# The same steps of a hand-ordered kernel in another order, from step 440 to about 1206

## The chip, the cores and the metric

The kernel runs on one core of a Trainium2 chip. The core has a matrix engine (PE, with a separate unit that loads weights, PEld), a vector engine (DVE), a scalar engine (ACT), a further engine for element-wise work (POOL, also called GpSimd), and SP, which issues the transfers. Each engine works through its own instructions in the order in which the program gives them, and an instruction that waits for another engine holds up all that stand behind it on its own engine. The metric is the time of one execution in microseconds (us). The profile reports a span, the time between the first and the last instruction, which is a little shorter.

## The reference

```python
def _attn_ref(x, a, B, C):                      # x (4, 8, 768, 32), B and C (4, 8, 768, 16)
    log_a = np.log(np.clip(a, 1e-06, 1.0))
    for c in range(nc):                         # chunks of 32 tokens
        cum = np.cumsum(la, axis=-1)
        L = np.exp(cum[:, :, :, None] - cum[:, :, None, :]) * causal
        CB = np.einsum('bhin,bhjn->bhij', Cc, Bc)
        y_intra = np.einsum('bhij,bhjd->bhid', CB * L, xc)
        y_inter = np.einsum('bhin,bhnd->bhid', Cc, state) * np.exp(cum)[:, :, :, None]
        y[:, :, sl] = y_intra + y_inter
        state = decay_full * state + np.sum(Bx, axis=2)
...
def _moe_ref(x, w_gate, w_val, w_out, rms_g):   # x (3072, 256), 256 -> 1536 -> 256
    rms = np.sqrt(np.mean(x * x, axis=-1, keepdims=True) + 1e-06)
    xn = x / rms * rms_g
    g = xn @ w_gate
    silu = g * (1.0 / (1.0 + np.exp(-g)))
    return (silu * (xn @ w_val) @ w_out)
```

A scan over chunks with a carried state (first function) gives y; heads and head elements of a token are put side by side as 256 features, and each token goes through a norm, a gated pair of projections to 1536, and a projection back to 256. All is float32.

## The kernel before

The 3072 tokens are worked on in six blocks (0 to 5) of 512. While the projections of one block run, the scan and the norm of the next block are computed beside them. The two projections of a block are made with a scheme of seven products in place of eight on 2 x 2 parts (half blocks of 256 tokens, pairs of 128-wide slices of the 1536 features, j = 0 to 5). The projection back is made with a fast scheme of twenty products on sums of the hidden values and sums of the weights. Block 0 has a plainer path of its own.

The whole program is a list of 1667 steps written out by hand in a string, `order`, of the form `block:kind.numbers`. A loop at the end of the function takes them one by one and calls the function of that kind, which emits its instructions. The list thus sets the order on every engine at once: two steps that use the same engine run there in the order of the list, and steps on different engines run beside each other as far as data and buffers allow. Nothing re-orders them later.

```python
    for step in order.split():
        ...
        if blk == "0":
            first_kinds[kind](*numbers)
        else:
            kinds[kind](int(blk), *numbers)
```

The kinds that the text uses, with their lines:

- `P.k.j` (L965, `product_gv`): product k of the seven for pair j, on PE: four matmuls of 128x256 into one of two pairs of PSUM banks, "gate" and "val", two passes each; it reads the normed tokens `xn` or their differences `tx`. `take.k.j` (L971) is the ACT copy of the gate bank after product 1, 6 or 7; the next product that adds onto this bank waits for it. `C.c.j` (L977, DVE) adds the copy to the val bank; `silu.c.j` (L215, ACT) applies the gate function; `hid.c.j` on DVE or `hidp.c.j` on POOL (L990) multiplies into the hidden values.
- `u.n` on DVE or `up.n` on POOL (L1060): the n-th of 16 sums of hidden values. `O.k.h` (L1086): half h of product k of the twenty, four matmuls of 128x128 on PE. `w.n` (L1113 a copy on ACT, L215 a negated copy on ACT, L1117 an addition on DVE) brings a product into the output tile `ob`; `put` (L1122, SP) stores 128 rows of it. `o.f` (L997) is the plain projection back of block 0, eight PE instructions each, for f = 0 to 11.
- The scan of the next block: `T`, `Tt`, `Td` (L558 DVE, L1194 ACT, L587 DVE) make turned operands, `g` (L613) their products on PE, `L` and `L1` (L646) their decay on DVE, `S` (L692 to L702) the states on DVE, `y` (L750, L678) the outputs on PE. `spread` (L514, SP) loads decays, `sub` or `subp` (L520, DVE or POOL) subtracts, `ex` (ACT with two masks on POOL, L507) is the exponential, `scale2` or `scale2p` (L539) scales, `bc`, `x` and `sq2` (SP) load, `dT` (L580, SP) loads decays for `Td`.
- The norm of the next block: `sq` (squares on ACT, L215, then an addition on POOL, L802), `yt` (ACT copies of y, L818 and L821), `ms` (sums over the features on PE, L834), `rs` (root on ACT and its store, "roots", L847), `rb` (four loads that spread it over the partitions, L852), `xn` (two DVE operations, L861), `tx` or `txp` (differences, L942, DVE or POOL). For these steps the block number is that of the block whose projections run: `1:ms` is the norm of block 2.
- `two` or `twop` (L1042), `cw` or `cwp` (L934): sums of weights on DVE or POOL. ACT holds one set of functions at a time; going from silu to exponential and logarithm or back emits a table load (L207 to silu, L209 to exponential). `exps` and `table` ask for one early.

The sums and the factors of the twenty products are tables; where a p follows a kind's name, the same operation is handed to POOL:

```python
    def sum_h(blk, n, engine=nc.vector):
        o, in0, in1 = SUMS[n]
        engine.tensor_tensor(out=hidden_or_sum(o), in0=hidden_or_sum(in0),
        ...
        "u": sum_h, "up": lambda blk, n: sum_h(blk, n, nc.gpsimd), "O": product_o, "w": total_o, "put": put_tile,
```

Of the kernel before, what the change touches and what calls it, by code (L numbers as in the profile page):

```python
# [20 lines left out]
def kernel(  # L21
# [1231 lines left out]
    def of_chunk(n, fn):  # L1253
# [79 lines left out]
        1:Tt.1.0 1:Td.1 1:C.12.3 0:sq2.2.0.3 1:T.0.0 1:Td.0 1:hidp.12.0 1:spread.1 1:hid.11.2 0:o.10
        1:P.3.2 1:bc.0 1:T.1.0 1:take.1.5 1:scale2p.0 1:sq2.1.0 1:C.12.2 1:sq2.1.3 0:o.11
        1:silu.12.3 1:two.10 1:P.6.5 2:bc.0 1:P.6.4 0:put.0 1:silu.12.2 1:P.2.4 0:put.3 1:C.11.4
        0:put.2 1:hid.12.2 0:put.1 1:P.2.5 1:take.6.4 1:P.7.4 1:P.5.4 1:take.6.5 1:C.11.5 1:take.7.4
        1:silu.11.4 1:P.7.5 1:take.7.5 1:g 1:sq2.0.0 1:P.4.5 2:bc.1 1:P.5.5 1:hid.22.2 1:silu.11.5
        1:sub.2 1:hid.12.3 1:C.22.4 1:hid.11.4 1:P.4.4 1:two.6 1:subp.1 1:silu.21.5 1:sub.0
        1:hid.11.5 1:silu.22.4 1:hidp.22.4 1:L1.3 1:hid.21.5 1:up.1 1:O.2.0 1:O.2.1 1:twop.7
        1:C.22.5 1:L 1:silu.22.5 1:O.15.0 1:silu.21.4 1:L1.2 1:P.3.5 1:hid.21.4 1:O.15.1 1:y.0 1:w.0  # L1340
        1:w.2 1:sq2.0.1 1:up.0 1:O.3.0 2:dT.0 1:sq2.0.3 1:C.12.5 1:silu.12.5 1:hid.12.5 1:sq2.1.1
        1:u.3 1:O.3.1 1:O.0.0 1:O.0.1 1:P.3.4 1:w.4 1:u.2 1:sq2.1.2 1:O.17.0 1:O.17.1 1:w.5 2:S.0
        1:O.6.0 1:O.6.1 1:u.4 1:u.5 1:u.9 1:up.6 1:w.10 1:x.1 1:C.12.4 1:O.16.0 1:silu.12.4
        1:hid.12.4 1:hid.22.5 1:u.7 1:O.4.0 1:O.4.1 1:sq2.0.2 1:O.9.0 1:O.9.1 1:u.10 1:O.16.1 1:ex.0
# [7 lines left out]
        2:sub.3 1:ex.1 1:ex.2 1:w.25 2:scale2.1 2:take.1.1 2:ex.3 2:P.6.1 2:C.11.0 2:P.2.1  # L1352
        2:take.6.0 2:P.7.0 2:C.11.1 2:L 2:take.6.1 2:P.7.1 2:take.7.0 2:silu.11.1 2:L1.3 1:put.0
        2:P.5.1 2:take.7.1 2:C.22.1 2:dT.1 2:Td.1 2:L1.2 2:P.4.0 2:silu.21.0 2:P.5.0 2:C.22.0
        2:silu.11.0 2:spread.0 2:P.4.1 2:silu.21.1 2:silu.22.0 2:hidp.22.0 2:hid.21.1 2:P.3.1
        2:C.12.1 2:hid.21.0 2:y.0 2:P.1.3 2:take.1.3 2:P.1.2 2:hid.11.1 2:take.1.2 2:P.3.0
        2:hid.11.0 2:silu.22.1 2:C.12.0 2:silu.12.0 1:put.1 2:hid.12.0 2:silu.12.1 2:hidp.12.1
        2:P.2.3 3:scale2p.1 2:C.11.3 2:silu.11.3 2:P.6.3 2:take.6.3 2:P.6.2 3:S.0 3:dT.1 2:P.2.2
        2:C.11.2 2:sq2.1.3 2:sq2.0.0 2:take.6.2 2:P.5.3 2:silu.11.2 2:P.7.2 2:take.7.2 1:put.3
        2:table 2:P.7.3 2:hid.11.2 2:P.5.2 2:C.22.2 2:hid.11.3 2:take.7.3 2:P.4.2 2:silu.21.2  # L1360
        2:sq2.1.2 1:put.2 2:hid.21.2 2:P.4.3 2:C.22.3 2:silu.22.3 2:hid.22.3 2:silu.21.3 2:sq2.1.1
        3:T.0.1 2:silu.22.2 2:hid.22.2 2:x.1 2:y.1 3:S.1 2:sq 2:yt 2:P.1.5 2:hid.21.3 2:P.3.2
# [18 lines left out]
        3:sq2.0.1 2:w.19 3:silu.21.0 3:hid.22.0 3:P.4.1 3:scale2.0 3:silu.21.1 3:sq2.1.1 3:L1.3
        2:w.21 2:w.24 3:hid.21.0 3:silu.11.0 2:w.23 2:O.10.0 2:O.10.1 3:P.2.1 2:w.25 3:hid.21.1
        4:dT.1 3:C.11.1 3:P.1.4 3:take.1.4 3:P.1.3 3:L1.2 3:y.0 3:P.5.1 3:sub.1 3:C.22.1 3:take.1.3
        3:P.6.3 3:P.2.3 3:silu.22.1 3:hidp.22.1 3:silu.11.1 2:put.3 3:take.6.3 3:P.3.1 3:P.6.4
        3:P.7.3 3:silu.12.0 3:hid.12.0 3:C.11.3 3:silu.11.3 3:hid.11.3 3:C.12.1 3:P.5.3 3:hid.11.0
        4:T.1.1 3:take.6.4 3:P.7.4 3:take.7.3 3:C.22.3 3:P.2.4 3:P.4.3 3:silu.12.1 3:hid.12.1
        3:take.7.4 3:P.4.4 3:x.1 3:P.3.3 3:silu.22.3 3:C.11.4 3:hid.11.1 3:silu.21.4 4:S.0
        3:silu.21.3 2:put.2 3:C.12.3 3:silu.12.3 3:hidp.12.3 3:table 3:hid.21.4 3:hid.21.3
        3:silu.11.4 3:P.5.4 3:y.1 3:subp.3 3:P.1.5 3:C.22.4 3:silu.22.4 3:take.1.5 3:hidp.22.4
        3:hid.22.3 4:S.1 3:P.1.2 3:P.3.4 3:take.1.2 3:C.12.4 3:sq 3:silu.12.4 3:sq2.0.2 3:P.6.5  # L1390
        3:take.6.5 3:P.2.5 2:put.0 4:T.0.1 4:Tt.0.1 3:C.11.5 3:P.2.2 3:C.11.2 3:yt 3:P.6.2
        3:take.6.2 3:silu.11.2 3:hid.11.4 3:P.7.5 3:P.5.5 3:take.7.5 3:silu.11.5 3:hidp.12.4 2:put.1
        3:C.22.5 3:silu.22.5 3:P.7.2 3:hid.11.2 3:take.7.2 3:P.4.5 3:silu.21.5 3:u.0 3:P.5.2 3:P.4.2
        3:hidp.22.5 4:Tt.0.0 3:hid.21.5 3:hid.11.5 3:O.2.0 3:sq2.0.3 3:O.2.1 3:O.15.0 3:C.22.2
        3:silu.21.2 3:O.15.1 3:hid.21.2 3:P.3.2 3:silu.22.2 3:u.1 3:u.3 3:C.12.2 3:P.3.5 3:C.12.5
        3:u.4 3:hid.22.2 3:w.0 3:w.2 3:O.3.0 3:O.3.1 3:O.0.0 4:Tt.1.1 3:silu.12.2 4:T.1.0 3:up.2
        3:O.0.1 3:hidp.12.2 3:O.6.0 3:silu.12.5 3:ms 3:w.4 3:O.17.0 3:O.17.1 3:rs 3:w.5 3:w.10
        3:hidp.12.5 3:O.6.1 3:up.5 3:rb 3:O.16.0 3:O.16.1 3:u.6 4:Tt.1.0 3:w.1 3:w.3 3:u.7 3:u.8
# [93 lines left out]
```

## Time and profile before

| | before |
|---|---|
| median of 3 runs | 392.15 us (392.1 to 392.5) |
| profiled execution, its own time | 392.46 us |
| its span | 390.6 us |
| matmul instructions, and their weight loads | 3805 and 3805 |
| instructions on DVE, ACT, POOL | 620, 471, 160 |
| bytes read and written in HBM | 23.69 MB, 3.74 MB |

The costliest groups of instructions on each engine but PE are these (line, engine, operation, operands, shapes, count; busy time in the span and mean ns of one; idle time of the engine just before them and what ended most of it):

```profile
L977 DVE TENSOR_TENSOR c<-val,p 128x512 f32<-128x512 f32 x99 | 67.6, 687 | 46.8 <-PE val L965 32.3
L971 ACT COPY p<-gate 128x512 f32<-128x512 f32 x99 | 57.0, 582 | 60.5 <-PE gate L965 58.4
L990 POOL TENSOR_TENSOR hid<-c 128x256 f32<-128x256 f32 x33 | 26.8, 814 | 94.0 <-ACT c L215 79.1
```

Idle time of an engine that others wait for matters; idle time of DVE, ACT or POOL that PE does not wait for costs nothing. So the views to read are those of PE: its busy share, what it waits for, the chain of waits that leads back from the last instruction, and the timeline around the places where one block's norm must be ready for the next block's first products.

### The profile page before, as it was taken

How to read it: one execution, taken by the hardware profiler on the slowest of the kernel's cores; microseconds unless marked ns; L12 is line 12 of the kernel's file. 1: busy time of each engine (PE TensorE's matmuls, PEld its weight loads, DVE VectorE, ACT ScalarE, POOL GpSimd, SP SyncE). 2: the span in 40 equal slices, each digit the busy share in tenths (PEclk: the TensorE clock that was granted, in tenths of full speed). 3: DMA queues.
4: the chain of work that ended last, by engine and by line, in shares of the span. 5: the costliest groups of instructions: out<-in, count | busy, mean ns of one | idle time of the engine just before them, and what ended most of it. 6: DMA issues, size and time to landing. Idle time of an engine off the chain costs nothing.

```text
span 390.6 us, 9632 instructions
## 1 busy us (share of the span) xinstructions
PE 383.9 (98%) x3805; PEld 329.0 (84%) x3805; DVE 290.4 (74%) x620; ACT 227.2 (58%) x471; POOL 140.7 (36%) x160
## 2 busy tenths in 40 slices
...
DMA packets 109940, 28.05 MB, mean 72 GB/s; under 512 B 94824, under 2 KB 103752, under 8 KB 109896
## 3 DMA queue, kind: packets, MB, share of 16 engines
...
q8 instruction: 30, 0.49, 0.6%
...
HBM read 23.69 MB, written 3.74 MB: 70 GB/s over the span
## 4 chain that ended last, share of the span: by engine, by line
PE 87%; DVE 9%; issue 2%; DMA 1%; ACT 0%; POOL 0%; DVEq 0%; POOLq 0%
PE gate L965 29%; PE o L1086 22%; PE val L965 22%; PE o L997 5%; PE y L750 3%; PE g L613 1%; DVE wgv L243 1%; DVE m L237 1%; DVE m L234 1%; DVE hid L912 1%; PE g L606 1%; PE e L474 1%; PE y L678 1%; DMA L<-rowd 1%; DVE L L652 1%
## 5 line engine op out<-in xcount | busy, mean ns | idle before, releaser
L977 DVE TENSOR_TENSOR c<-val,p 128x512 f32<-128x512 f32 x99 | 67.6, 687 | 46.8 <-PE val L965 32.3
L971 ACT COPY p<-gate 128x512 f32<-128x512 f32 x99 | 57.0, 582 | 60.5 <-PE gate L965 58.4
L965 PE MATMUL gate<-tx,wgv 128*128 128x256 f32 x264 | 65.5, 381 | 0.0
L990 POOL TENSOR_TENSOR hid<-c 128x256 f32<-128x256 f32 x33 | 26.8, 814 | 94.0 <-ACT c L215 79.1
L215 ACT ACTIVATE c<-c 128x256 f32<-128x256 f32 x99 | 39.8, 415 | 31.8 <-DVE c L977 31.7
L965 PEld LDWEIGHTS gate<-tx,wgv 128*128 128x128 f32 x264 | 49.3, 190 | 7.5 <-ACT p L971 1.0
L990 DVE TENSOR_TENSOR hid<-c 128x256 f32<-128x256 f32 x66 | 32.5, 500 | 9.7 <-ACT c L215 9.5
L1117 DVE TENSOR_TENSOR ob<-ob,o 128x128 f32<-128x128 f32 (+1 forms) x90 | 24.3, 297 | 19.7 <-PE o L1086 13.7
L1086 PE MATMUL o<-two,hid 128*128 128x128 f32 x280 | 36.7, 277 | 0.0
L1086 PEld LDWEIGHTS o<-two,hid 128*128 128x128 f32 x280 | 34.6, 192 | 1.2 <-issue 0.4
L965 PE MATMUL val<-tx,sw 128*128 128x256 f32 x132 | 34.0, 381 | 0.0
L965 PE MATMUL val<-xn,wgv 128*128 128x256 f32 x132 | 33.3, 380 | 0.0
L965 PE MATMUL val<-xn,sw 128*128 128x256 f32 x132 | 33.3, 380 | 0.0
L965 PE MATMUL gate<-tx,sw 128*128 128x256 f32 x132 | 33.0, 381 | 0.0
L965 PE MATMUL gate<-xn,wgv 128*128 128x256 f32 x132 | 32.9, 384 | 0.0
L507 POOL TENSOR_SCALAR_AFFINE_SELECT L<-L 64x512 f32<-64x512 f32 x32 | 23.3, 729 | 21.0 <-ACT L L215 19.7
L965 PEld LDWEIGHTS val<-tx,sw 128*128 128x128 f32 x132 | 24.7, 190 | 3.7 <-DVE c L977 0.2
L965 PEld LDWEIGHTS val<-xn,wgv 128*128 128x128 f32 x132 | 24.9, 190 | 3.4
L965 PEld LDWEIGHTS gate<-tx,sw 128*128 128x128 f32 x132 | 24.5, 190 | 3.8 <-ACT p L971 0.4
L965 PEld LDWEIGHTS gate<-xn,wgv 128*128 128x128 f32 x132 | 24.0, 190 | 3.9 <-DVE hid L912 0.3
L965 PEld LDWEIGHTS val<-xn,sw 128*128 128x128 f32 x132 | 24.4, 190 | 3.2 <-issue 0.2
L215 ACT ACTIVATE e<-e,kinks 128x512 f32<-128x512 int16 (+1 forms) x36 | 26.0, 722 | 1.2
...
## 6 DMA issues: line engine op xcount, KB each, us to landing
...
```

The source lines that it names most:

```text
L215: nc.scalar.activation(**operands)
L234: nc.vector.tensor_scalar(out=m, in0=hi, scalar1=0xFFFFF, scalar2=0x100000, op0=ALU.bitwise_and, op1=ALU.bitwise_or)
L237: nc.vector.scalar_tensor_tensor(out=f, in0=lo.bitcast(U32), scalar=2.0 ** -32, in1=m, op0=ALU.mult, op1=ALU.add)
L507: nc.gpsimd.affine_select(out=L[r], in_=L[r], pattern=[[0, L.shape[1]], [1, HC]], compare_op=ALU.is_ge, fill=0.0, base=0, channel_multipli ...
L750: nc.tensor.matmul(out=y[2 * k + u][rows, (2 * n + i) * HC:(2 * n + i + 1) * HC], start=(k, u, rows.start) not in opened, stop=True, skip_ ...
L965: nc.tensor.matmul(out=dst[:, half[w]], lhsT=lhsT, rhs=rhs, start=(k in (1, 2, 5) and w == 0), stop=True, skip_group_check=True)
L971: nc.scalar.copy(out=t, in_=Xs[j])
L977: nc.vector.tensor_tensor(out=t, in0=Zs[j], in1=a, op=ALU.add)
L990: engine.tensor_tensor(out=hid[:, 2 * j + c // 10 - 1, c % 10 - 1], in0=u, in1=src[:, half[1]], op=ALU.mult)
L997: nc.tensor.matmul(out=o, lhsT=hid[:, f, k // 2, (k % 2) * P:(k % 2 + 1) * P], rhs=wo[:, f], start=opens, stop=(f == NF - 1), skip_group_c ...
L1086: nc.tensor.matmul(out=Os[blk, b][:, place * P:(place + 1) * P], lhsT=hidden_or_sum(u)[:, g], rhs=rhs, start=(blk, b) not in opened, stop= ...
L1117: nc.vector.tensor_tensor(out=o, in0=o, in1=src, op=ALU.add if what[0] == "+" else ALU.subtract)
```

## The change

Only the string `order` changes. Its first 439 steps and those from the 1207th on stand as they were. The steps between (from block 1's later projections to block 4's first ones) are the same set in another order, which was made with the lengths of the operations varied a little at random. Of these 767 steps 58 also change the engine that does them: 33 go from DVE to POOL (17 `u`, 6 `hid`, 4 `sub`, 3 `tx`, a `cw`, a `two`, a `scale2`) and 25 from POOL to DVE (8 `hid`, 7 `u`, 3 `sub`, 3 `scale2`, 3 `tx`, a `two`). The 107 P, 114 O, 5 o, 3 g, 6 y and 3 ms steps of the part and the 251 transfers of the whole kernel are the same in kind and number. The steps 0:o.7 to 0:o.11, spread up to the 505th place before, all stand before the 469th after. In parts, with what is left out marked by "...":

```diff
-        1:w.1 3:bc.1 1:y.1 1:w.6 1:w.3 2:T.0.1 2:Tt.0.0 1:u.11 2:S.1 1:O.18.0 1:O.18.1 1:u.12
-        1:O.8.0 1:O.8.1 1:w.11 1:O.13.0 1:O.13.1 1:sq 1:yt 2:T.0.0 2:spread.2 1:ms 2:scale2p.0 1:rs
-        1:w.12 1:w.7 1:w.8 1:w.16 2:spread.3 0:exps 1:w.13 1:O.11.0 1:u.8 1:O.11.1 1:O.12.0 1:O.12.1
-        1:up.14 1:O.5.0 1:O.5.1 1:w.9 1:w.18 2:T.1.1 2:Tt.1.0 1:w.20 1:O.1.0 1:O.7.0 1:O.7.1 1:rb
-        2:T.1.0 1:w.17 1:w.15 2:Tt.1.1 1:up.13 1:O.1.1 1:w.22 2:Tt.0.1 1:w.14 1:w.19 1:xn 2:g
-        1:O.14.0 2:x.0 1:O.14.1 1:O.19.0 1:O.19.1 1:tx.0 2:sq2.1.0 1:up.15 1:w.24 1:O.10.0 1:O.10.1
-        2:P.1.0 2:take.1.0 1:w.21 2:P.1.1 1:w.23 1:txp.1 1:tx.2 1:tx.3 2:P.2.0 2:P.6.0 2:Td.0
...
-        2:P.5.5 2:silu.22.4 2:hidp.22.4 2:silu.21.5 2:hid.21.5 3:spread.3 2:ms 2:O.2.0 2:hid.11.4
-        2:silu.21.4 3:x.0 2:O.2.1 3:subp.0 3:dT.0 2:O.15.0 2:O.15.1 2:rs 2:hid.21.4 2:C.22.5 2:P.3.5
...
+        2:Tt.1.0 1:O.4.1 1:O.9.0 1:O.9.1 1:u.10 1:w.3 1:w.6 1:up.11 1:y.1 2:T.0.1 2:Tt.0.0 2:S.1
+        1:O.18.0 1:O.18.1 1:sq 1:sq2.0.2 1:yt 1:O.8.0 1:w.11 1:u.8 1:w.12 1:sq2.0.1 1:w.8 1:O.8.1
+        1:O.13.0 1:O.13.1 1:w.16 1:ms 1:rs 1:w.13 2:T.1.0 1:O.11.0 1:O.11.1 1:w.7 1:up.12 2:T.0.0
+        3:bc.1 1:ex.1 1:O.5.0 1:O.5.1 1:w.20 1:O.12.0 1:O.12.1 2:Tt.0.1 1:O.7.0 1:O.7.1 1:up.13
+        1:u.14 2:g 1:w.18 1:O.1.0 1:w.9 1:w.17 1:ex.2 1:O.1.1 1:w.15 1:w.14 1:O.14.0 1:O.14.1 2:Td.0
+        1:u.15 1:O.19.0 1:O.19.1 1:w.22 1:w.19 1:rb 1:O.10.0 1:O.10.1 2:scale2.1 1:xn 1:w.24 1:tx.0
+        1:txp.1 1:put.3 2:P.1.1 2:take.1.1 1:txp.2 2:spread.2 1:w.25 1:w.21 2:sq2.1.0 2:P.1.0
...
+        1:put.0 2:L1.3 2:subp.3 2:P.6.3 2:dT.1 2:C.12.1 2:spread.1 2:silu.11.2 2:x.0 2:hid.11.2
+        1:put.2 2:ex.3 2:P.6.2 2:take.6.2 3:dT.1 2:Td.1 2:take.6.3 2:hid.11.0 2:sq2.0.0 2:y.0
+        2:P.2.3 2:C.11.3 2:sq2.1.2 2:silu.11.3 2:P.7.2 3:scale2.1 2:P.7.3 2:take.7.3 2:take.7.2
...
+        2:P.5.4 2:C.22.4 2:silu.11.4 2:yt 2:silu.22.4 3:subp.0 3:spread.3 2:P.4.5 2:P.4.4
+        2:silu.21.4 2:P.5.5 2:ms 2:hid.11.4 2:hid.21.4 2:hidp.12.2 2:O.2.0 2:hidp.22.4 2:up.0
+        2:O.2.1 2:O.15.0 2:silu.21.5 2:hid.21.5 2:C.22.5 2:O.15.1 3:exps 2:P.3.5 2:sq2.0.2
+        3:spread.2 2:up.1 2:exps 2:u.3 2:up.4 2:rs 2:rb 3:T.1.0 3:T.0.0 2:ex.1 2:w.0 2:P.3.4 2:w.2
+        2:O.3.0 2:C.12.5 2:C.12.4 3:sq2.1.0 2:silu.22.5 3:sq2.1.3 2:O.3.1 2:O.0.0 2:silu.12.5
+        3:Tt.0.1 2:hid.12.5 2:O.6.0 2:O.6.1 2:O.16.0 2:O.16.1 2:w.1 2:hid.22.5 2:up.5 2:table
+        2:O.0.1 3:spread.1 2:silu.12.4 3:g 2:w.4 2:u.2 2:xn 2:O.17.0 2:w.3 2:O.17.1 2:w.5 2:w.10
+        3:P.1.0 3:P.2.0 2:hidp.12.4 2:u.9 2:txp.0 2:ex.0 2:tx.2 2:O.4.0 3:take.1.0 2:up.6 2:up.7
...
```

More of the change, by code (lines that the diff above doesn't have):

```diff
@@ L1333 @@
[L1333 to L1344, printed above, removed]
@@ L1351 @@
-        2:P.1.0 2:take.1.0 1:w.21 2:P.1.1 1:w.23 1:txp.1 1:tx.2 1:tx.3 2:P.2.0 2:P.6.0 2:Td.0
[L1352 to L1362, printed above, removed]
@@ L1381 @@
[L1381 to L1392, printed above, removed]
@@ L1393 @@
[L1393 to L1398, printed above, removed]
@@ L1446 @@
-        5:u.12 5:w.20 5:O.12.0 5:O.7.0 5:O.7.1 5:up.13 5:w.14 5:w.9 5:O.12.1 5:w.17 5:w.18 5:w.15
-        5:put.3 5:u.14 5:O.1.0 5:O.1.1 5:w.19 5:put.0 5:O.14.0 5:u.15 5:w.22 5:O.14.1 5:O.19.0
-        5:O.19.1 5:w.21 5:w.23 5:put.1 5:O.10.0 5:O.10.1 5:w.24 5:w.25 5:put.2
+        1:P.7.3 0:sq2.2.1.3 0:ex.11 1:two.11 1:take.7.3 0:sq2.2.1.1 1:T.0.1 0:o.7 0:o.8 1:P.5.3
+        1:ex.3 1:hidp.22.1 1:silu.12.0 0:sub.8 1:P.4.3 1:silu.21.3 1:silu.11.3 1:T.1.1 1:hid.12.0
+        0:ex.8 1:P.7.2 1:two.5 1:two.10 1:hid.11.3 1:cwp.2.3 0:sq2.2.0.1 1:C.22.3 0:o.9 0:o.10
@@ new lines @@
+        0:o.11 1:P.5.2 1:P.3.3 1:silu.22.3 0:sq2.2.0.3 1:bc.0 1:scale2.0 1:take.7.2 1:Tt.0.1
+        1:sq2.1.0 1:hid.21.3 1:subp.2 1:twop.7 1:spread.1 1:T.1.0 1:silu.11.2 1:Tt.0.0 1:bc.1
+        1:P.4.2 1:silu.21.2 1:C.22.2 1:C.12.3 1:hidp.22.3 1:silu.12.3 1:hidp.12.3 1:x.0 1:subp.1
+        1:hid.21.2 1:P.1.4 1:take.1.4 1:P.2.4 1:C.11.4 1:T.0.0 2:bc.0 1:P.3.2 1:Tt.1.1 1:P.6.4
+        2:bc.1 1:C.12.2 1:P.1.5 1:Tt.1.0 0:put.0 0:put.3 1:hid.11.2 1:P.2.5 1:Td.1 0:put.2
+        1:take.6.4 0:put.1 1:take.1.5 1:C.11.5 1:silu.11.5 1:silu.12.2 1:scale2.1 1:hid.12.2 1:P.7.4
@@ new lines @@
+        1:P.6.5 1:take.7.4 1:silu.11.4 1:P.5.4 1:take.6.5 2:dT.0 1:P.4.4 1:silu.21.4 1:twop.6
+        1:two.9 1:sq2.1.1 1:C.22.4 1:hid.11.5 1:sq2.0.0 1:g 1:hid.11.4 1:silu.22.4 1:Td.0 1:P.7.5
+        1:hid.21.4 1:P.5.5 1:silu.22.2 1:L 1:sq2.1.2 1:O.2.0 1:L1.3 1:take.7.5 1:hidp.22.4 1:P.4.5
+        1:C.22.5 1:L1.2 1:O.2.1 1:O.15.0 1:O.15.1 1:silu.22.5 1:u.0 1:hid.22.5 1:y.0 1:hid.22.2
+        1:silu.21.5 1:w.0 1:hid.21.5 1:u.1 1:P.3.5 1:u.2 1:w.2 1:O.3.0 1:O.3.1 1:O.0.0 1:O.0.1 1:w.4
+        1:P.3.4 1:O.17.0 1:C.12.5 1:silu.12.5 1:O.17.1 1:w.5 2:S.0 2:scale2.0 1:hid.12.5 1:w.10
@@ new lines @@
+        2:silu.22.3 2:hidp.22.3 2:P.5.2 2:C.22.2 2:sq2.1.3 2:P.4.3 2:y.1 3:S.1 2:sq 2:P.4.2
+        2:silu.21.2 2:P.3.3 2:hid.21.2 2:C.12.3 2:silu.21.3 2:hid.21.3 2:hid.11.3 2:silu.12.3
+        2:P.3.2 1:put.1 2:P.1.5 2:take.1.5 2:silu.22.2 3:T.1.1 3:Tt.1.1 2:C.12.2 2:hidp.12.3
+        2:silu.12.2 2:P.1.4 2:sq2.0.3 2:hid.22.2 3:T.0.1 2:take.1.4 2:P.2.5 2:C.11.5 2:silu.11.5
+        2:hid.11.5 3:spread.0 3:Tt.0.0 2:P.6.5 2:take.6.5 2:P.6.4 2:take.6.4 2:P.2.4 2:C.11.4
+        2:P.7.5 2:take.7.5 3:dT.0 2:P.7.4 2:spread.0 2:subp.0 3:Tt.1.0 3:Td.1 2:take.7.4 2:sq2.0.1
@@ new lines @@
+        3:L1.2 3:sq2.1.2 2:up.11 2:up.12 3:subp.2 2:O.7.1 3:sub.3 3:sq2.0.0 3:silu.12.0 2:O.11.0
+        2:O.11.1 3:sq2.0.1 2:O.12.0 2:up.13 2:O.12.1 2:w.17 2:w.15 3:P.7.1 3:take.7.1 2:w.18 2:w.14
+        3:hid.21.0 2:u.14 3:table 2:O.1.0 2:O.1.1 2:w.22 3:silu.11.0 2:up.15 2:O.14.0 2:O.14.1
+        2:O.19.0 2:O.19.1 3:P.4.1 3:silu.21.1 3:sq2.1.1 2:w.19 2:O.10.0 2:O.10.1 3:hid.22.0 2:w.23
+        2:w.24 2:w.25 3:P.1.3 3:P.2.1 3:take.1.3 2:w.21 4:dT.0 3:Td.0 3:C.11.1 3:hid.21.1 3:x.0
+        3:bc.0 3:P.2.3 3:subp.1 3:silu.11.1 2:put.3 3:scale2p.0 3:P.6.3 3:hid.12.0 3:hid.11.1
@@ new lines @@
+        3:C.12.4 3:hid.22.4 3:P.6.5 3:take.6.5 3:P.2.5 3:C.11.5 3:silu.12.4 3:hid.12.4 2:put.2
+        3:silu.11.5 3:P.6.2 3:take.6.2 2:put.0 3:P.7.5 4:S.0 3:x.1 3:y.1 3:P.7.2 3:P.5.5 3:C.11.2
+        3:hid.11.5 3:take.7.5 3:P.4.5 3:silu.11.2 3:take.7.2 3:up.0 4:S.1 3:sq 3:C.22.5 3:P.4.2
+        3:silu.21.5 4:T.1.1 4:Tt.1.0 3:hid.21.5 3:silu.21.2 3:hid.11.2 3:hid.21.2 4:T.0.0 3:P.5.2
+        3:C.22.2 3:u.3 2:put.1 3:up.1 3:up.4 3:up.2 3:yt 3:silu.22.2 3:hid.22.2 3:O.2.0 3:O.2.1
+        3:O.15.0 3:O.15.1 4:T.1.0 3:w.0 3:w.2 3:P.3.5 3:C.12.5 3:silu.22.5 3:silu.12.5 3:P.3.2
@@ new lines @@
+        4:silu.12.1 4:P.1.3 4:silu.12.0 4:silu.22.0 4:hidp.22.0 4:take.1.3 4:L1.2 4:P.2.2 4:P.6.2
+        4:P.6.3 4:L1.3 4:take.6.2 4:take.6.3 4:hid.12.0 4:L 4:C.11.2 4:P.2.3 4:P.7.2 4:C.11.3
+        4:silu.11.3 4:hid.11.3 4:silu.11.1 4:P.7.3 4:P.5.3 4:take.7.3 4:silu.11.2 4:C.22.3
+        4:hid.11.2 4:take.7.2 4:P.5.2 3:put.1 4:C.22.2 4:silu.22.2 4:P.4.3 4:silu.21.3 4:hid.21.3
+        4:silu.22.3 4:hid.11.1 4:P.4.2 4:silu.21.2 4:P.3.3 4:C.12.3 4:silu.12.3 4:hid.21.2
+        4:hidp.22.3 4:P.1.4 3:put.3 4:hid.12.3 4:y.0 4:y.1 4:P.1.5 4:take.1.4 4:take.1.5 4:P.6.4
@@ new lines @@
+        4:hid.22.2 4:take.6.4 4:P.3.2 4:C.12.2 4:P.6.5 4:silu.12.2 4:take.6.5 4:P.2.5 4:hidp.12.1
+        4:P.2.4 4:C.11.5 4:sq 4:P.7.5 4:silu.11.5 4:take.7.5 4:C.11.4 4:P.7.4 4:P.5.4 4:silu.11.4
+        4:hid.12.2 3:put.2 4:take.7.4 4:P.4.5 4:P.5.5 4:hid.11.4 4:C.22.4 4:silu.22.4 4:hidp.22.4
+        4:silu.21.5 4:hid.21.5 4:hid.11.5 4:u.1 4:P.4.4 4:silu.21.4 4:hid.21.4 4:yt 4:C.22.5 4:up.0
+        4:O.2.0 4:O.2.1 4:O.15.0 4:u.3 4:u.4 4:O.15.1 3:put.0 4:silu.22.5 4:ms 4:P.3.5 4:w.0 4:w.2
+        4:O.3.0 4:O.3.1 4:O.0.0 4:C.12.5 4:silu.12.5 4:O.0.1 4:hid.22.5 4:O.6.0 4:w.4 4:P.3.4 4:u.2
```

127 lines of the change are left out of this document (59 added, 68 removed).

## The prediction, made before the changed kernel had run

> **What bounds the kernel now.** I read the page first, then the busy time in stretches of 10 us, PE's waits, the chain of waits, and the timeline around the norms of blocks 1 and 2.
>
> ```profile
> span 390.6 us, 9632 instructions
> PE 383.9 (98%) x3805; PEld 329.0 (84%) x3805; DVE 290.4 (74%) x620; ACT 227.2 (58%) x471; POOL 140.7 (36%) x160
> ...
> PE 87%; DVE 9%; issue 2%; DMA 1%; ACT 0%; POOL 0%; DVEq 0%; POOLq 0%
> ```
>
> PE is busy for 98% of the span and is 87% of the chain. The reordered steps run from about 103 to 272.7 us. Their stretches, and PE's waits in them:
>
> ```profile
> core 0: us, PE busy (x) PEld busy (x) DVE busy (x) ACT busy (x) POOL busy (x), PEclk, DMA share, GB/s
> ...
> 132.00:142.00 10.00, 10.00 (x266) 9.43 (x268) 8.56 (x21) 3.95 (x10) 3.22 (x4) 1.00 0.39 49
> 142.00:152.00 10.00, 9.30 (x160) 8.55 (x161) 6.77 (x23) 5.78 (x15) 6.06 (x6) 1.00 0.25 84
> ...
> sum 170.00, PE 169.30 PEld 151.30 DVE 127.32 ACT 95.28 POOL 72.51; mean PE 9.96 PEld 8.90 DVE 7.49 ACT 5.60 POOL 4.27
> ```
>
> ```profile
> PE ms L834 <- POOL sq L802: 0.7, 1, 0.7
> ```
>
> The clock is 1.00 in each row. Of 170 us, PE stands visibly idle for 0.70 us, before the norm sums of block 1 (1:ms). A short wait hides in the rows as a matmul that ends a little late, so I price PE's work by undisturbed groups of the chain:
>
> ```profile
> 103.31 0.93 PE val L965 x4
> ...
> 109.42 3.45 PE o L997 x16
> ...
> 151.78 1.14 PE g L613 x63
> ...
> 184.28 0.97 PE gate L965 x4
> ...
> 194.56 1.98 PE o L1086 x16
> ...
> 208.45 2.68 PE o L1086 x24
> ...
> 271.88 1.73 PE gate L965 x8
> ```
>
> ```profile
> 141.15 0.49 PE L750 MATMUL y<-T,S 32*64 32x64 f32 x32
> ...
> 142.67 0.60 PE L1086 MATMUL o<-sw,hid 128*128 128x128 f32 x3
> ```
>
> A P step is 1.73/2 = 0.865 us, an O step 2.68/6 = 0.447, an o step 3.45/2 = 1.725, a g 1.14, a y 142.67 − 141.15 = 1.52, an ms 0.43. The part holds 107 P, 114 O, 5 o, 3 g, 6 y and 3 ms: 92.6 + 51.0 + 8.6 + 3.4 + 9.1 + 1.3 = 166.0 us. The part begins at 103.31; its last P before the unchanged tail ends half way through the 271.88 group, at 272.74: 169.4 us. So **no order of this part can gain more than about 3.4 us**: the 0.70, and some 2.7 of small losses like the 0.97 beside 0.865 and the 1.98 beside 1.79.
>
> **What the change does.** The same 1667 steps are issued; 767 of them stand elsewhere, and 58 of these on another engine: 33 from DVE to POOL, 25 back. PE's steps are the same in kind and number, so PE's work stays at 166.0 and only its waits can change. What the other engines do lies beside PE except where a wait shows.
>
> *Block 1, y.1 to ms.*
>
> ```profile
> 143.22 1.15 ACT L215 ACTIVATE sq<-y 128x256 f32<-128x256 f32 x3 [0.27 <-DVE A L692]
> 144.51 1.75 POOL L802 TENSOR_TENSOR sq<-sq 128x512 f32<-128x512 f32 x1 [1.00 <-DMA L<-rowd]
> 146.31 0.43 PE L834 MATMUL ms<-sq,mean 128*32 128x128 f32 x8 [0.70 <-POOL sq L802]
> ...
> 147.54 0.35 SPq L847 DMA_DIRECT2D roots<-r  x1
> 147.70 1.07 DVE L1117 TENSOR_TENSOR ob<-ob,o 128x128 f32<-128x128 f32 x4 [2.01 <-ACT ob L1113]
> 149.14 1.93 SPq L852 DMA_DIRECT2D sq<-roots  x4
> 152.76 2.48 DVE L861 SCALAR_TENSOR_TENSOR xn<-yt,gcol,sq 128x512 f32<-128x512 f32 x2
> 152.77 1.27 POOL L1060 TENSOR_TENSOR hid<-hid 128x512 f32<-128x512 f32 x1
> ...
> 155.63 1.89 PE L965 MATMUL gate<-xn,wgv 128*128 128x256 f32 x8
> ```
>
> ACT's squares and POOL's addition take from 143.22 to 146.26. Both orders put six O steps (2.68 us) on PE between y.1 and ms, so the wait stays. In block 2 the same POOL addition took 1.28 instead of 1.75; if it does here too, 0.48 is gained. Term: 0 (−0.5 to 0).
>
> *Block 1, ms to the next block's first product.* 16 O and a g, 8.29 us, follow ms in both orders. Before, rs waits on ACT for ms with w.12 behind it, and DVE waits 2.01 us for that w.12; the O steps that reuse the bank come late by about a tenth each. After, w.12 stands ahead of rs. PE takes 155.63 − 146.31 − 0.43 = 8.89 us for that 8.29, so 0.6 can go here, and with faster following pieces 1.0; the chain root, four loads, xn (152.76 + 2.48 = 155.24, 0.39 before the product) limits it. Term: −0.4 (−1.0 to 0).
>
> *Block 2, around ms.*
>
> ```profile
> 183.47 0.67 ACT L818 COPY yt<-y 128x256 f32<-128x256 f32 x2
> 183.68 1.28 POOL L802 TENSOR_TENSOR sq<-sq 128x512 f32<-128x512 f32 x1 [9.46 <-ACT sq L215]
> 184.15 1.17 ACT L821 COPY yt<-y 64x512 f32<-64x512 f32 x2
> ...
> 193.78 1.28 ACT L209 ACT_TABLE_LOAD   x1
> 195.48 0.31 ACT L215 ACTIVATE r<-r 128x128 f32<-128x128 f32 x1
> ...
> 197.40 3.31 SPq L852 DMA_DIRECT2D sq<-roots  x4
> ...
> 202.48 0.63 ACT L215 ACTIVATE L<-L 128x512 f32<-128x512 f32 x1
> 202.60 1.80 DVE L861 SCALAR_TENSOR_TENSOR xn<-yt,gcol,sq 128x512 f32<-128x512 f32 x2 [0.91 <-DMA sq<-roots]
> 203.91 1.03 PE L965 MATMUL gate<-xn,wgv 128*128 128x256 f32 x4
> ```
>
> ```profile
> L971 ACT COPY p<-gate 128x512 f32<-128x512 f32 x46 | 26.5, 582 | 27.1 <-PE gate L965 25.0 <-DVE c L977 1.2 <-ACT c L215 0.8
> L215 ACT ACTIVATE c<-c 128x256 f32<-128x256 f32 x49 | 19.9, 415 | 14.4 <-DVE c L977 14.3
> L1060 DVE TENSOR_TENSOR hid<-hid 128x512 f32<-128x512 f32 x11 | 7.5, 688 | 0.2
> L1060 POOL TENSOR_TENSOR hid<-hid 128x512 f32<-128x512 f32 x6 | 8.4, 1407 | 6.9 <-DVE s L1060 3.4 <-PE o L1086 3.3
> ```
>
> Before, the two yt copies (0.67 + 1.17) come right after the squares, ten products ahead of ms. After, yt stands behind P.5.4's silu.11.4, with silu.22.4 behind it: 1.84 + 0.42 = 2.26 us of ACT against the 1.73 of P.4.5 and P.4.4, so silu.21.4 starts up to 0.5 late. It and hid.21.4 (by the 415 ns rows, 0.8 together) are due before O.2.0, 0.865 + 0.43 = 1.3 us after P.4.4: no margin is left. I take +0.2 (0 to 0.5). Further on a silu load (1.28) stands ahead of silu.12.4, and so of its hid, and O.6.1's inputs come behind one more copy and a silu (0.58 + 0.42): +0.25 (0 to 0.5). An exp load, copies and silus ahead of rs make the root about 0.7 later than now; xn waits 0.91 for the loads' data already, while xn's first half (202.60 to about 203.5) leaves near 0.4 to the product at 203.91. xn stands earlier in PE's order after (O.0.1 and g just before it), so part of 0.7 may show: 0 taken, up to +0.7. Together: **+0.45** (0 to 1.7).
>
> *Block 2's P phase* gets one exp (2:ex.3) with its two loads between the copies take.1 and take.6: 1.28 + 0.63 + 1.28 = 3.2 us of ACT by the rows. Behind ex.3 stand take.6.2 and take.6.3 (0.58 each); the first must be done before P.7.2, which P.6.2, y.0 and P.2.3 (0.865 + 1.52/2 or more + 0.865) put about 1.7 after P.6.2's end. ACT can be about 0.4 late without a loss. Term: 0 (0 to 0.9). The Trainium skill, page "ScalarE: Activation LUTs", section "What ACT_TABLE_LOAD costs", gives each switch a drain of about 1.38 us behind the load of 1.28, which would make the pair 2.8 us dearer and, by estimate, this term about 2 us. The trace speaks against it: the load at 193.78 ended at 195.06 and the root's chain ran its two steps by 195.79.
>
> *Block 3:* 9.8 instead of 9.4 us of PE's work lie between ms and the next block's first product; its first sums wait no longer by rows. 0 (−0.3 to 0.5). *Elsewhere,* some 40 of 206 PE waits had margins under 0.5 us before and the new order has other such places: 0 (±0.6).
>
> Sum: 0 − 0.4 + 0.45 + 0 + 0 + 0 = +0.05 us on 392.46, the profiled execution's own time (1.9 over its span). That is 0.31 above the median of 392.15; on the median it gives **392.2**.
>
> **The rivals.**
>
> *Faster: the norm chain of block 1 shortens.* POOL's addition at 1.28 gives −0.48, and xn at 1.80, as in block 2, instead of 2.48 lets the next product start earlier; with the term of −0.4 at its bound of −1.0 and block 2 at +0.2, the sum is −1.3: 391.1 from the profiled time, 390.9 from the median. For it: 0.7 of idle is really there, and o.7 to o.11, which need nothing from block 1, are only used earlier. Against: both distances on PE are equal.
>
> *Slower: POOL takes sums that PE waits for.* Sums in the part go from 32 on DVE and 16 on POOL to 22 and 26. A POOL sum takes 1.41 against DVE's 0.69, so one on the path costs 0.72. And where the two run together both are slow: xn's two halves took 2.48 at 152.76 with POOL's sum beside it, 1.80 alone at 202.60. From the point at which three or more of the ten lie on a path with no margin (those of block 2's output phase have 0.4 to 0.9 by distance), it costs 3 × 0.72 + 0.2 = +2.3: 394.5. For it: POOL's chains in block 2's output phase are long. Against: PE's waits of before name POOL once. The Trainium skill, page "SBUF — State Buffer", section "Who interferes with whom", makes it a rule: a DVE operation with two inputs in SBUF contends with a GpSimd operation that reads SBUF, the second one blocking for the whole of the first. The 2.48 beside 1.80 fits a partial block; by a full one xn would have come 1.27 later, not 0.68.
>
> *Slower: xn of block 2 is late.* The root 0.7 later, a product that waits for xn, and the margin of about 0.4 used up by O.2.0's wait give +0.45 + 0.7 = +1.2: 393.3. For it: the 0.91 wait for the loads. Against: g now stands between.
>
> *It does more or less than another order.* 58 steps change engine; but PE's 98% makes either thing worth little, which is the forecast.
>
> **How the numbers follow.** The forecast gets 0.42, faster 0.23, POOL's sums 0.20, the late xn 0.15. About 0.2% (0.78 us) is what a measurement tells from no change: same 0.42, faster 0.23, slower 0.35. The likeliest's own range is 391.4 to 393.0. The range takes in the faster rival (390.9) and the slower one (394.5), a little beyond each: 390.7 to 394.8.
>
> **What would show it.** In the changed profile: a PE wait at ms of 0.2 to 0.7; w.12's copy ahead of the root and the piece from ms to 2:P.1.0 near 8.9 − 0.4; in block 2 O.2.0 late behind hid.21.4 and xn still waiting for the loads; POOL named before PE nowhere but at ms. The prediction is wrong if PE's idle in the part passes 2 us, if sums on POOL release PE, or if the stretch from 103 to the tail is over 1 us shorter or longer.

## The result, and the profile after

| | before | after |
|---|---|---|
| median of 10 runs each | 392.34 us (391.66 to 392.61) | 390.79 us (390.31 to 391.79) |
| ratio, 95% interval | | 0.9966 (0.9958 to 0.9975) |
| profiled execution, its own time | 392.46 us | 391.25 us |
| its span | 390.6 us | 389.5 us |

The changed kernel is faster by 0.34%, about 1.3 us (1.0 to 1.6 by the interval; the two medians lie 1.55 apart, the two traces 1.31 by the table below); no change was forecast. Of the page of the changed kernel, the lines that answer to those of before (span; busy time of each engine; shares of the chain that ended last):

```profile
span 389.5 us, 9637 instructions
PE 383.3 (98%) x3805; PEld 329.8 (85%) x3805; DVE 289.8 (74%) x612; ACT 226.4 (58%) x471; POOL 152.0 (39%) x168
...
PE 87%; DVE 9%; issue 2%; ACT 1%; DVEq 0%; ACTq 0%
```

The busy time by stretches of 10 us:

```profile
core 0: us, PE busy (x) PEld busy (x) DVE busy (x) ACT busy (x) POOL busy (x), PEclk, DMA share, GB/s
...
142.00:152.00 10.00, 9.99 (x223) 9.20 (x202) 8.67 (x25) 6.52 (x18) 7.39 (x7) 1.00 0.28 55
...
sum 170.00, PE 169.85 PEld 152.90 DVE 128.27 ACT 95.58 POOL 84.10; mean PE 9.99 PEld 8.99 DVE 7.55 ACT 5.62 POOL 4.95
```

POOL has 11.6 us more to do in the part (84.1 against 72.5), DVE about as much as before (128.27 against 127.32), and PE is held up less: 169.85 of 170 against 169.30, and the list of PE's waits in the part, which had 0.7 for ms, has no entry. The timeline of the changed kernel around block 1's norm:

```profile
141.29 0.49 PE L750 MATMUL y<-T,S 32*64 32x64 f32 x32
...
142.84 0.49 DVE L692 TENSOR_TENSOR A<-y,tmask 128x128 f32<-128x128 f32 x2
...
143.18 1.14 ACT L215 ACTIVATE sq<-y 128x256 f32<-128x256 f32 x3
...
144.40 1.31 POOL L802 TENSOR_TENSOR sq<-sq 128x512 f32<-128x512 f32 x1 [0.86 <-ACT sq L215]
144.49 0.28 DVE L1117 TENSOR_TENSOR ob<-ob,o 128x128 f32<-128x128 f32 x1
144.69 1.06 PE L1086 MATMUL o<-two,hid 128*128 128x128 f32 x8
144.69 1.56 DVE L1060 TENSOR_TENSOR s<-hid 128x512 f32<-128x512 f32 x1
...
145.76 0.43 PE L834 MATMUL ms<-sq,mean 128*32 128x128 f32 x8
...
153.60 1.41 DVE L861 SCALAR_TENSOR_TENSOR xn<-yt,gcol,sq 128x512 f32<-128x512 f32 x2
...
154.79 1.46 PE L965 MATMUL gate<-xn,wgv 128*128 128x256 f32 x6
```

POOL's addition took 1.31 us instead of 1.75, and ms follows it with no open wait. DVE's sum beside it, u.8 here, took 1.56 where such a sum takes 0.69 alone. In the kernel before it was the other way round; the sum u.12, which the prediction did not look at, stands on DVE just ahead of the addition at 144.51:

```profile
144.45 0.68 DVE L1060 TENSOR_TENSOR hid<-hid 128x512 f32<-128x512 f32 x1
```

Where the gain lies is read best by steps. Each row of PE was put to its step by the order of the program; the table gives the time from the start of 1:P.7.3, the last step of PE that stands at the same place in both orders ahead of the changed part, to the start of the step named (for "first P" whichever of P.1.0 and P.1.1 comes first).

| from 1:P.7.3 to | before | after | the stretch that ends here, after minus before |
|---|---|---|---|
| 1:y.1 | 38.87 | 38.80 | -0.07 |
| 1:ms | 44.03 | 43.28 | -0.68 |
| first P of block 2 | 53.34 | 52.31 | -0.28 |
| 2:ms | 91.86 | 90.27 | -0.56 |
| first P of block 3 | 101.62 | 100.25 | +0.22 |
| first P of block 4 | 166.78 | 165.41 | 0.00 |
| 4:P.6.0, unchanged tail | 170.30 | 168.93 | 0.00 |
| end of the trace | 288.29 | 286.98 | +0.06 |

1.03 us are gained up to the first product of block 2, 0.68 of it between y.1 and ms; a further 0.34 net come from block 2, none from block 3 or the tail.

### The profile page after: what moved, and what is told of

Read it like the earlier page. It is cut to its first block, busy times and chain, and to the rows that moved or that the text cites. A ratio compares the mean times of both kernels' runs of the same rounds, so it can differ in the third digit from the quotient of the medians.

```text
span 389.5 us, 9637 instructions
## 1 busy us (share of the span) xinstructions
PE 383.3 (98%) x3805; PEld 329.8 (85%) x3805; DVE 289.8 (74%) x612; ACT 226.4 (58%) x471; POOL 152.0 (39%) x168
## 4 chain that ended last, share of the span: by engine, by line
PE 87%; DVE 9%; issue 2%; ACT 1%; DVEq 0%; ACTq 0%
PE gate L965 29%; PE o L1086 23%; PE val L965 21%; PE o L997 5%; PE y L750 3%; PE g L613 1%; DVE wgv L243 1%; DVE m L237 1%; DVE m L234 1%; DVE hid L912 1%; PE g L606 1%; PE e L474 1%; PE y L678 1%; DVE L L652 1%; ACT yt L821 0%
## 5 line engine op out<-in xcount | busy, mean ns | idle before, releaser
L990 POOL TENSOR_TENSOR hid<-c 128x256 f32<-128x256 f32 x31 | 24.7, 800 | 87.1 <-ACT c L215 83.1
L990 DVE TENSOR_TENSOR hid<-c 128x256 f32<-128x256 f32 x68 | 34.5, 521 | 6.9 <-ACT c L215 6.7
```

Source lines behind the costliest of these rows:

```text
L990: engine.tensor_tensor(out=hid[:, 2 * j + c // 10 - 1, c % 10 - 1], in0=u, in1=src[:, half[1]], op=ALU.mult)
```

## The experiments

The theory to be tested: most of the gain is made where block 1's norm starts, by which of two operations, DVE's sum or POOL's addition, is issued first, and the rest by steps that no longer stand ahead of what PE needs next. The rivals: DVE's lighter load makes it (58 steps run on another engine), or it is spread in small waits over the part. All times by step below are from 1:P.7.3, as in the table.

**One sum later (e1).**

```diff
-2:S.1 1:O.18.0 1:O.18.1 1:u.12 1:O.8.0 ... 2:T.0.0 2:spread.2 1:ms
+2:S.1 1:O.18.0 1:O.18.1 1:O.8.0 ... 2:T.0.0 1:u.12 2:spread.2 1:ms
```

> The kernel before with one step moved: block 1's sum u.12 on DVE, which began at 144.45 (0.06 before POOL's addition of the squares), stands behind 2:T.0.0 instead. Theory (order of issue at the norm of block 1): POOL's addition takes about 1.3 instead of 1.75, PE's wait at ms falls from 0.70 to 0.2 to 0.35, the first product of block 2 (2:P.1.0) starts near 155.2 instead of 155.63, and the time falls by 0.4 (ratio 0.999). u.12 itself is slow in its place (over 1.2 instead of 0.68). Rival (the gain comes from DVE's lighter load, spread over the part): the addition may change, but the time does not move beyond 0.1. Rival (small waits elsewhere): no change either.

Its timeline:

```profile
144.69 1.27 POOL L802 TENSOR_TENSOR sq<-sq 128x512 f32<-128x512 f32 x1 [1.01 <-ACT sq L215]
145.18 1.32 DVE L1060 TENSOR_TENSOR hid<-hid 128x512 f32<-128x512 f32 x1
146.01 0.42 PE L834 MATMUL ms<-sq,mean 128*32 128x128 f32 x8 [0.23 <-POOL sq L802]
```

The addition takes 1.27, u.12 1.32, the wait is 0.23; ms comes at 43.54, 0.49 earlier, and all behind it with it (end 287.82, -0.47). The runs give 0.9991 (0.998 to 1.0002), which agrees and alone would not separate it from no change.

**One copy earlier (e2), and both moves (e3, the third run).**

```diff
-1:sq 1:yt 2:T.0.0 2:spread.2 1:ms 2:scale2p.0 1:rs 1:w.12
+1:sq 1:yt 1:w.12 2:T.0.0 2:spread.2 1:ms 2:scale2p.0 1:rs
```

> The kernel before with one step moved: the ACT copy w.12 of block 1 stands right behind yt, ahead of rs, as in the changed kernel. Theory: DVE's wait of 2.01 for this copy goes, of the six late O steps between ms and 2:P.1.0 two to four go (0.1 each), PE needs 8.6 to 8.7 instead of 8.89 from the end of ms to 2:P.1.0, the wait at ms stays at 0.7, and the time falls by 0.2 to 0.3 (ratio 0.9994). Rival (the O steps are late because of their own sums or weights, not the copy): DVE's wait goes, PE keeps its 8.89, time unchanged.

> Both moves of the two runs before together. Theory: they add up, since the chain of the norm and the O steps shift together: about -0.4 - 0.25 = -0.65 to the first product of block 2 (near 155.0), ratio near 0.9983. Rival (the later chain root, loads, xn decides when 2:P.1.0 starts): the second saving does not arrive, 2:P.1.0 starts at 155.2 and the wait stands there, for xn.

The copy alone: ms stays at 44.02, the stretch from ms to the first P falls from 9.31 to 9.14, the end comes at 288.12, 0.17 earlier: a little under what was expected; the runs (1.0002, 0.9991 to 1.0013) can't see it. Both moves: ms at 43.56, first P at 52.70, end 287.65: -0.64 in the trace, so the two add up and xn was not the limit. The runs give 0.9992 (0.998 to 1.0004). The "most" of the theory is too much: the order at the addition makes 0.49 of the 1.31, both moves 0.64.

**Two neighbours on DVE exchanged (e13).** A sharper form of e1: u.12 is only put behind the addition w.11.

```diff
-1:O.18.1 1:u.12 1:O.8.0 1:O.8.1 1:w.11
+1:O.18.1 1:w.11 1:u.12 1:O.8.0 1:O.8.1
```

> The kernel before with two neighbours on DVE exchanged: block 1's w.11 (an addition with one operand in PSUM, 0.28) ahead of the sum u.12 (both operands in SBUF, 0.68). Theory (whichever of DVE's sum and POOL's addition is issued first goes on, the other waits for it): u.12 now begins about 0.2 later, behind POOL's addition instead of 0.06 ahead of it; the addition takes 1.3 instead of 1.75, u.12 1.3 or more instead of 0.68, the wait at ms falls from 0.70 to 0.2 to 0.3, the rest moves up with it, and the end comes 0.4 to 0.5 earlier in the trace (ratio near 0.999). Rival (the two share the port evenly, both slow whatever the order): the addition stays near 1.75 and nothing is gained.

```profile
143.09 1.15 ACT L215 ACTIVATE sq<-y 128x256 f32<-128x256 f32 x3 [0.27 <-DVE A L692]
144.39 1.27 POOL L802 TENSOR_TENSOR sq<-sq 128x512 f32<-128x512 f32 x1 [1.01 <-ACT sq L215]
144.53 1.68 DVE L1060 TENSOR_TENSOR hid<-hid 128x512 f32<-128x512 f32 x1
145.71 0.42 PE L834 MATMUL ms<-sq,mean 128*32 128x128 f32 x8 [0.21 <-POOL sq L802]
```

u.12 now starts 0.14 behind POOL's addition instead of 0.06 ahead of it. The addition goes through in 1.27; u.12 ends at 146.21, 0.55 after the addition's end at 145.66. In e1, e3, e9, e13 and the changed kernel the sum began 0.14 to 0.83 behind the addition, and each time it ended 0.54 to 0.55 after the addition's end: it hardly moves until the addition is through. End 287.80, -0.49, and here the runs separate it: 0.9987 (0.9978 to 0.9995). Even sharing, where both are slow whatever the order, is ruled out.

**The squares earlier (e9).** e3, with a transpose and a mask step that stood ahead of 2:S.1 moved behind yt.

```diff
-1:y.1 1:w.6 1:w.3 2:T.0.1 2:Tt.0.0 1:u.11 2:S.1 1:O.18.0
+1:y.1 1:w.6 1:w.3 1:u.11 2:S.1 1:O.18.0 ... 1:sq 1:yt 2:T.0.1 1:w.12 2:Tt.0.0 2:T.0.0 1:u.12
```

> The kernel before with both moves of the third run (u.12 behind 2:T.0.0, w.12 behind yt) and 2:T.0.1 and 2:Tt.0.0 set behind yt. Theory (ACT's squares of block 1 start late because the additions of 2:S.1, which they wait for, stand behind u.11 and a transpose on DVE): the additions start 0.2 earlier after y.1, the squares too, and the wait at ms goes from the 0.22 of that run to 0.05 or less; from 1:P.7.3 to 4:P.6.0 the trace takes 169.4 to 169.5 against 169.66 there and 170.30 before. Rival (the squares wait for PE's y.1 alone): the wait stays at 0.2.

```profile
142.30 0.47 DVE L692 TENSOR_TENSOR A<-y,tmask 128x128 f32<-128x128 f32 x2
142.61 1.15 ACT L215 ACTIVATE sq<-y 128x256 f32<-128x256 f32 x3 [1.22 <-DVE A L692]
...
145.23 0.43 PE L834 MATMUL ms<-sq,mean 128*32 128x128 f32 x8
```

The open wait at ms is gone; ms comes at 43.48, 0.08 before e3's, 4:P.6.0 at 169.58. That misses the 169.5 expected at most by 0.08, though the mechanism is there: the squares start when DVE's additions are done. The runs give 0.9979 (0.9971 to 0.9988).

**yt of block 2 later (e12).**

```diff
-2:y.1 3:S.1 2:sq 2:yt 2:P.1.5 ... 2:P.5.4 2:take.7.4 2:C.22.4
+2:y.1 3:S.1 2:sq 2:P.1.5 ... 2:P.5.4 2:take.7.4 2:yt 2:C.22.4
```

> The kernel before with block 2's yt (four ACT copies, 1.84) moved from right behind the squares to behind take.7.4, near ms, as in the changed kernel. Theory (before, these copies hold up the takes of P.1.5, P.6.5 and others, each costing PE about 0.1; near ms they hold up O.2.0's inputs): the stretch from 2:P.1.0 to 2:ms falls from 38.52 by 0.3 to 0.5, that from 2:ms to 3:P.1.0 grows from 9.76 by 0.1 to 0.4: net -0.3 to 0. Rival (the late takes come from DVE or from the table loads): the first stretch stays within 0.1 of 38.52.

PE's waits in it between 185 and 200 us (what waits, what ends it; us in total, times, longest):

```profile
PE o L1086 <- DVE hid L990: 0.2, 1, 0.2
```

The stretch from the first P to 2:ms takes 38.20 instead of 38.52, that from 2:ms to the next first P 9.99 instead of 9.76: the step frees copies that it stood in front of (P.6.5 and P.7.5 are no longer 0.1 late each; P.1.5, which was also expected to be freed, still is) and delays O.2.0 in its new place, net -0.1. The runs agree with that and with nothing: 0.9998 (0.999 to 1.0007).

**Half of the change (e4, e5).** The list of one kernel up to block 2's first products, then the steps that are left in the other's order.

```diff
 e4: changed order from 1:P.7.3 ... 2:P.1.0 | rest in the order of before
 e5: order of before up to 2:P.1.1 | rest in the changed order
```

> The changed order from step 440 up to block 2's first products (2:P.1.0), then the steps that are left in the order of before. Theory (most of the gain is made in block 1): 2:P.1.1 starts near 154.8 as in the changed kernel, and 0.8 to 1.0 of the gain of 1.2 in the trace is there, time near 391.1 to 391.5. Rival (the gain is spread over the whole part, by engine shares and small waits): a third or less of it, 391.9 or more. A junction of two orders can bring a wait of its own; it would show between 155 and 165.

> The order of before up to block 2's first products (2:P.1.1), then the steps that are left in the changed order. Theory: the wait of 0.70 at ms and the late O steps of block 1 stay, and only some 0.2 to 0.4 is gained in block 2: 391.8 to 392.2. Rival (spread gain): two thirds or more, 391.3 or less.

PE's waits just behind the junction, first of e4, then of e5:

```profile
PE gate L965 <- ACT p L971: 1.1, 2, 0.6
```

```profile
PE gate L965 <- POOL tx L942: 3.1, 1, 3.1
```

Both missed in time: 1.0031 (1.002 to 1.0043) and 1.0142 (1.0121 to 1.0164), for the junctions cost more than was to be found. By steps, e4 still says what it was made for: first P at 52.30, the whole -1.03 of block 1 (1.04 here), then 1.55 lost up to 2:y.1 (25.83 from the first P against 24.28 before), and from there to 4:P.6.0 92.68, the same as before. e5 keeps the stretches of before up to its junction and loses 5 us at it; it settles nothing about block 2. Not all of the 5 is the wait of 3.1: right behind it the granted clock falls (PEclk, the last column but two), and the clock's record has half speed from 161.04 to 164.45, which by estimate is another 1.7 (the 4.30 us busy there hold 12 matmuls, the next 5.00 hold 25).

```profile
core 0: us, PE busy (x) PEld busy (x) DVE busy (x) ACT busy (x) POOL busy (x), PEclk, DMA share, GB/s
155.00:160.00 5.00, 2.57 (x12) 1.91 (x11) 2.19 (x7) 3.81 (x6) 2.70 (x5) 1.00 0.58 174
160.00:165.00 5.00, 4.30 (x12) 3.47 (x13) 0.56 (x1) 0.78 (x2) 1.33 (x2) 0.66 0.42 49
165.00:170.00 5.00, 5.00 (x25) 4.41 (x24) 2.54 (x5) 2.25 (x6) 0.00 (x0) 1.00 0.04 5
```

**The engines apart from the order (e6, e7).** Each order with the other kernel's engine for the 58 steps, as in

```diff
 e6, the changed order:
-1:hidp.22.1 ... 1:two.5 ... 1:up.3
+1:hid.22.1 ... 1:twop.5 ... 1:u.3
 e7, the order of before: the same the other way round
```

> The changed kernel's order with the engine of before for each of the 58 steps that had changed theirs. Theory (the gain is order at block 1's norm, not the engines' shares): the wait at ms stays under 0.2 and the time within 0.4 of the changed kernel (390.5 to 391.2), unless a moved sum meets the addition again. Rival (lighter DVE makes it): the gain goes, 391.9 to 392.6.

> The order of before with the changed kernel's engine for each of the 58 steps. Theory: no gain; POOL's longer sums stand in places that were not made for them, -0.2 to +1.5 (392.2 to 393.8), and the wait at ms stays 0.5 or more. Rival (lighter DVE makes it): 391.0 to 391.5.

Both missed by far: 407.88 us, 1.0398 (1.0369 to 1.0426) of the kernel before, and 406.71 us, 1.0366 (1.0344 to 1.0387). By the traces that is 17.1 more than the changed kernel, whose order e6 has, and 14.9 more than the kernel before, whose order e7 has. The first entries of e6's list of waits, PE's over the span, and one of DVE's between 100 and 150 us:

```profile
PE val L965 <- DVE c L977: 3.2, 1, 3.2
PE o L1086 <- POOL hid L1060: 2.5, 2, 2.0
PE o L1086 <- DVE ob L1117: 2.4, 2, 2.0
```

```profile
DVE sw L1042 <- POOL two L1042: 8.2, 1, 8.2
```

Each swap alone loses, so neither order nor engines can be called the cause of the whole gain without the other; the changed kernel's engines as such (e7) bring nothing, and DVE's load in the part had not fallen (128.27 against 127.32). A chain handed to the slower engine in a place made for the faster one stops the in-order queue behind it, here DVE for 8.2 us. Here too the clock adds a little: in the traces it was granted at half for 3.41 us twice in e6 and once in e7, by estimate 3.4 and 1.7 us; two of e7's five runs kept a clock of 1.0 and still took 404.82 and 405.90.

**The tail (e8, the eighth run), and more of it (e10).** Both kernels share a loss in block 5: O.1.0 waits 0.4 for a DVE addition, w.18, queued behind three others.

```diff
 e8, on the changed kernel:
-5:O.5.1 5:up.8 5:u.12 5:w.20 ... 5:O.12.1 5:w.17 5:w.18 5:w.15
+5:O.5.1 5:up.8 5:u.12 5:w.18 5:w.20 ... 5:O.12.1 5:w.17 5:w.15
 e10, on e8:
-2:yt 2:silu.22.4 ... 2:silu.21.4 2:P.5.5 ... 5:up.13
+2:yt ... 2:silu.21.4 2:silu.22.4 2:P.5.5 ... 5:u.13
```

> The changed kernel with one step moved in the unchanged tail: block 5's w.18 (the DVE addition that frees the bank of product 11) stands right behind u.12 instead of behind w.14, w.9 and w.17. In both traces O.1.0 of block 5 waits for it: the O step ahead of it (12.1) is 0.54 late, and 0.38 of that is an open wait for DVE. Theory: that wait goes and the end comes 0.4 to 0.7 earlier, 390.1 to 390.4. Rival (the stores and additions at the very end decide): the O steps move up, the end does not, 390.8.

> The changed kernel with three things: w.18 of block 5 behind u.12 (as in the eighth run), block 5's sum 13 on DVE instead of POOL (0.69 instead of 1.27, since that run showed O.14.0 waiting for it), and block 2's silu.22.4 behind silu.21.4 instead of ahead of it. Theory: O.14.0's wait goes (another 0.2 to 0.3 beside the 0.27 of that run), and O.2.0 of block 2 comes 0.2 earlier: the trace takes 286.2 to 286.4 from 1:P.7.3 to the end against 286.98 for the changed kernel; time near 389.7 to 390.0. Rival (the very end, additions and stores, decides, and block 2's lost 0.2 is met again at the next norm): 286.7 as in that run.

In e8 the step behind O.12.1 comes 0.45 after it instead of 0.99, the end at 286.71 instead of 286.98; half of it is lost again, since O.14.0 now waits for POOL's sum (1.27 at 381.64):

```profile
381.53 0.02 POOLq L1060
381.54 0.07 issue
381.61 1.31 POOLq L1488
382.92 0.04 issue
382.96 2.07 PE o L1086 x16
```

These five are pieces of e8's chain of waits (POOLq is POOL's sequencer; its piece of 1.31 is the time of the sum). e8 ran 390.06 us, 0.9957 (0.9945 to 0.9969) of before: the fastest, though only the trace, not the intervals, sets it ahead of the changed kernel. e10 was a miss: 391.40 us, 0.9982 (0.9971 to 0.9992), and 287.20 to the end of the trace, 0.22 later than the changed kernel. O.2.0 of block 2 came on time, but the sums behind the later hid came later too (2:ms to the next first P 10.24 instead of 9.98), and with the sum on DVE O.14.0 waited for DVE's additions behind it instead:

```profile
384.80 1.16 PE L1086 MATMUL o<-wo,s 128*128 128x128 f32 x8 [0.36 <-DVE ob L1117]
```

## Why the prediction was wrong, step by step

- **The bound held.** PE stayed at 98%, and up to 4:P.6.0 1.37 of the 3.4 us that any order could gain were gained. That is also beyond the 1 us by which the prediction let this stretch move.
- **Block 1, y.1 to ms: the step that failed.** "Both orders put six O steps (2.68 us) on PE between y.1 and ms, so the wait stays": 0 was taken and 0.5 allowed, -0.68 was measured, and the open wait foretold at ms (0.2 to 0.7) did not come. The distance on PE is equal; the chain beside it is not. 0.49 is the sum issued ahead of POOL's addition (e1, e13). The prediction had the row that tells it, 1.75 beside 1.28, and did not ask which DVE instruction ran at 144.45. The other 0.19 fits the squares: DVE reached 2:S.1's additions sooner after y.1, and ACT's squares with them (1.89 after y.1's first row instead of 2.07). No run isolates this in the changed kernel; e9 moved the same way with less, 0.08.
- **Block 1, ms to the next product:** -0.4 taken, -0.28 measured, of it 0.17 by w.12 (e2); the other 0.11 was not tried. Right, nearly in size too. The limit named for it, xn, was none: in the changed kernel the first product starts at 154.79, before xn's second half ends at 155.01 (153.60 + 1.41), so it needs the first half only.
- **Block 2, P phase: the second step that failed.** Only the exp pair was priced, at 0, and that was right: P.7.2 behind it starts at most 0.1 late, so the dearer pair that the prediction set aside (about 2 us) did not come either. But yt was costed only in its new place. Taking its 1.84 out from between the takes was worth 0.3 (e12), and the stretch gained 0.56. Most of the other 0.2 lies by steps at P.1.5 and P.1.4, 0.10 and 0.07 late before and in e12 and on time in the changed kernel; which step frees them was not tried.
- **Block 2, around ms:** +0.45 taken, +0.22 measured. O.2.0 behind hid.21.4 came as worked out, 0.2 late. O.6.1's 0.25 and the late xn did not come.
- **Block 3 and elsewhere:** 0 taken; block 3 measured 0.00, the steps up to 1:y.1 -0.07, the tail +0.06.
- **The rivals.** The faster one gave 390.9, and 390.79 was measured, but only its first price was the mechanism: POOL's addition 0.44 shorter. That its sum of -1.3 met the trace's -1.31 is luck: it has -1.0 between ms and the next product, where -0.28 came, and nothing in block 2's P phase, where -0.56 came. xn did become shorter, and nothing waited for that (e3). POOL's sums never made PE wait openly in the changed kernel. That an engine's change is "worth little" on a kernel at 98% is wrong as a reason: with the engines swapped in a fixed order it was 15 to 17 us (e6, e7).
- **The block by the other engine.** From 2.48 beside 1.80 the prediction read a partial block, with both operations slow. e13 shows a block that is full but for 0.13 us: whichever came first kept its 0.68 or 1.27, and the other took longer by most of the time that they shared (u.12 1.68, of which 1.13 inside the addition; before, the addition 1.75, of which 0.62 inside u.12). That is what the Trainium skill, page "SBUF — State Buffer", section "Who interferes with whom", says of two such operations: the one issued first has the pair of SBUF ports that the two engines share for the whole instruction, and issue order decides which one blocks. Read as a rule on order rather than on load, it would have priced this place at 0.5. The row of xn, on which the prediction set this rule aside, was misread. The 1.80 was no time alone: its second half ran beside a POOL mask and took 1.14 instead of 0.75. Undisturbed, the two halves take 1.41 (153.60 in the changed kernel). At 152.76 in the kernel before, one half took its usual 0.74 and the other 1.82, 1.08 more:

```profile
L861 DVE SCALAR_TENSOR_TENSOR xn<-yt,gcol,sq x2: 739/1280/1820, 152.8 to 154.5; 128x512 f32<-128x512 f32 x2
```

The long one, the first, ended at 154.58, again 0.55 after the end of POOL's operation at 154.03, and POOL kept its 1.27. So this row shows the same block. The profile has the two starts 0.01 apart, too close to say which was issued first.

The small sizes were near; the change was missed because two gains, 0.68 before block 1's norm sums (0.49 of it at the addition) and 0.56 in block 2's P phase (0.3 of it by yt), were entered as 0.
